# The last chunk of a weight stream: one load of 128 rows, or 14 loads of fewer than 16

## The chip, the cores and the metric

The kernel runs on one core of a Trainium2 chip. The metric is the device time of one execution in microseconds (us): 745.53 for the kernel before, the median of 3 runs (745.52 to 745.61).

## The reference

One decode step of a block in which attention and a gated layer stand side by side and are added to the residual, all in float32, for one token of 576 numbers:

```python
xn = _layernorm(x)
q = xn @ wq                                        # 32 heads of 128
p = softmax(einsum(q, k_cache) * 128 ** -0.5)      # 8192 cached keys for each head
A = einsum(p, v_cache).reshape(1, 1, 4096) @ wo    # 4096 x 576
gate, up = xn @ W_gate, xn @ W_up                  # 576 x 4608 each
h = gate * (gate > 0) * up
return x + A + h @ W_down                          # 4608 x 576
```

The caches are 2 x 32 x 8192 x 128 floats, 268 MB; with the weights the core reads 319 MB.

## The kernel before

Three big buffers of 128 partitions x 16384 floats (`slots`) are filled in turn by loads that SP issues in one queue, in the order in which they stand in `build`: the query weights, part of the gate weights, then for each head one load with its keys and the values of the head before it, then the last values with the rest of the gate weights (`vw`), and last the output weights (`wod`). VectorE multiplies the keys by the query and sums them (L292, L297), ScalarE takes the exponents (L311), and TensorE multiplies the values by them (L221). Each load waits until its buffer is free: `load` (L160) hands the waits to `add`, and `run` (L92) puts them ahead of the instruction on its engine.

The output stage multiplies one row by the 68 chunks of `wod`, each of 128 rows x 576 columns: 32 for the heads (`wo`), 36 for the gated layer (`W_down`). A chunk's rows lie on the 128 partitions, one row of 576 floats (2304 bytes) each. Chunks 0 to 8 come with `vw`. The others come in eight loads, whose sizes in chunks stand in `OUT` (L25): 28 into one buffer, 9, 7, 5, 4 and 3 into the next, 2 and 1 into the third. So the load of 3 brings chunks 62 to 64, that of 2 brings 65 and 66, and that of 1 brings chunk 67, the last. These two go into a buffer that is free when TensorE has done with the last head's values, with the gate products of the last part (`u3`) and with chunk 8 (`first`); SP's waits for all three are waits on TensorE's one counter, so one wait on the latest.

Each load has a semaphore of its own (`do65`, `do67`), to which a landed load has added 16; TensorE waits on it ahead of the first product of the load's first chunk (L404). Chunks 0 to 63 go in two halves each into the sums `acc`. When they are through, VectorE adds the residual (`y`, L422). The last four chunks go in four quarters each into `fin`; behind chunk 64 four products with `pick` bring `y` into the same sums, so TensorE waits for `y` there (L420). Then come chunks 65, 66 and 67, the copy of `fin` (L423) and the store of the 576 numbers (L185), which SP issues behind all loads.

In the profile, every matrix product and its weight load stand twice, as these are float32: the 4 products of a chunk's quarters are 8 rows. The 16 DMA engines that carry the loads aren't listed one by one; a view by stretches of time has their mean busy share.

Of the kernel before, what the change touches and what calls it, by code (L numbers as in the profile page):

```python
# [9 lines left out]
P = 128  # L10
D = 576
H = 32
# [4 lines left out]
FC = F // P  # L17
# [10 lines left out]
Q = D // 4  # L28

UNITS = (28, 32, 16, 5)  # L30


STEP = 16
# [4 lines left out]
class Program:  # L38
# [19 lines left out]
    def add(self, engine, f, waits=(), mark=None, on=None, by=1):  # L58
        to = None
        if mark is not None:  # L60
            to = on or engine
            self.sem(to)
            self.counts[to] += by
            assert mark not in self.marks, mark
            self.marks[mark] = (to, self.counts[to])
        self.lists[engine].append((f, tuple(waits), to, by))
# [41 lines left out]
def build(nc, x, kv, vw, wq, wqt, wg, wod, out):  # L108
    pr = Program(nc)
    add = pr.add  # L110

    def sb(name, shape):
        return nc.alloc_sbuf_tensor(name, list(shape), F32).ap()
# [4 lines left out]
    slots = [sb(f"slot{i}", [P, W]) for i in range(3)]  # L118
# [41 lines left out]
    def load(name, k, src, waits, on, start=0):  # L160
        dst = slots[k % 3][:, start:start + src.shape[-1]]
        add("sync", lambda e: e.dma_start(dst, src), waits, name, on=on, by=16)  # L162

    def tile(n):
        return slots[(n + 3) % 3]
# [11 lines left out]
    f = OUT[0][0]  # L177
    for k, loads in enumerate(OUT[1:]):
        free = ((("V", H - 3), ("mr", H - 2)), (("V", H - 2), ("mr", H - 1)), (("V", H - 1), "u3", ("first", OUT[0][0] - 1)))[k]
        i = 0  # L180
        for n in loads:
            load(("o", f), H + 4 + k, wod[:, (f - 9) * D:(f - 9 + n) * D], free, f"do{f}", i * D)
            i += n
            f += n
    add("sync", lambda e: e.dma_start(out.rearrange("o (j q) -> (o j) q", j=4), total4[0:P:32, :]), ("end",), "out", on="dout", by=16)  # L185
# [34 lines left out]
    def mm(waits, mark, o, lhsT, rhs, start, stop):  # L220
        add("tensor", lambda e: e.matmul(o, lhsT, rhs, start=start, stop=stop), waits, mark)  # L221
# [5 lines left out]
    for k in range(36):  # L227
        if k < 32:
            r, a, j = k // 16, k // 4 % 4, k % 4
# [25 lines left out]
    units += [(a, r, 0) for a in range(4) for r in (4, 5)] + [(4, 4, 0)]  # L255
    assert len(units) == sum(UNITS)
    first, last = {}, {}
# [5 lines left out]
    def gates(part):  # L263
        t, there = places[part]
        for u in range(UNITS[part]):
            k = sum(UNITS[:part]) + u
            a, r, j = units[k]
            mm((there, "qr") if u == 0 else (), f"u{part}" if u == UNITS[part] - 1 else None,
               bq[32 * j:32 * j + 32, :], xz[:, a, 5 - r:37 - r] if a < 4 else xt[:, 5 - r:37 - r],
# [71 lines left out]
    for n in range(1, H):  # L341
        k, i = (n - 1) // G, (n - 1) % G
# [52 lines left out]
    f, end = 0, H + FC  # L395
# [3 lines left out]
    for k, loads in enumerate(OUT):  # L399
        t = tile(H)[:, SK + UNITS[3] * 512:] if k == 0 else slots[(H + 3 + k) % 3]  # L400
        i = 0
        for n in loads:
            for m in range(n):
                waits = (("o", f),) if m == 0 and k else ()  # L404
                waits += needs.get(f, ())
                if f < end - LAST:
                    for j in range(2):
                        r = 64 * (f % 2) + 32 * j
# [75 lines left out]
```

## Time and profile before

| what | value |
|---|---|
| median of the runs | 745.53 us |
| the profiled execution, first to last instruction (span) | 744.4 us |
| read from HBM | 319.16 MB, 429 GB/s over the span |
| busy: PE, DVE, ACT | 40%, 78%, 5% of the span |
| issue of chunk 67's load to its landing | 25.9 us |
| copy of the result (L423) begins | 742.40 us |

Of the profiled execution the profile gives the span; the 1.1 us between it and the median lie around the first and the last instruction. PE is TensorE's products, PEld its weight loads, DVE VectorE, ACT ScalarE, SP the engine that issues the loads; an SPq row is the issue of a DMA. In a row of the timeline the first number is the start in us from the span's beginning, the second the time from the first to the end of the last of the instructions that were merged (x how many), and the bracket tells how long the engine had been idle before them and who let it go on.

### The profile page before, as it was taken

How to read it: one execution, taken by the hardware profiler on the slowest of the kernel's cores; microseconds unless marked ns; L12 is line 12 of the kernel's file. 1: busy time of each engine (PE TensorE's matmuls, PEld its weight loads, DVE VectorE, ACT ScalarE, POOL GpSimd, SP SyncE). 2: the span in 40 equal slices, each digit the busy share in tenths (PEclk: the TensorE clock that was granted, in tenths of full speed). 3: DMA queues.
4: the chain of work that ended last, by engine and by line, in shares of the span. 5: the costliest groups of instructions: out<-in, count | busy, mean ns of one | idle time of the engine just before them, and what ended most of it. 6: DMA issues, size and time to landing. Idle time of an engine off the chain costs nothing.

```text
span 744.4 us, 4100 instructions
## 1 busy us (share of the span) xinstructions
PE 296.1 (40%) x1772; PEld 86.0 (12%) x1772; DVE 577.1 (78%) x178; ACT 36.1 (5%) x113; POOL 2.1 (0%) x10
## 2 busy tenths in 40 slices
PE   1554413252343343343344334324324324334676
PEld 1111100010010010010010001001001001001122
DVE  2000189989999999999999999999999999999610
ACT  1000001010010010010000000001001000000000
POOL 1000000000000000000000000000000000000000
PEclk9967755656565565666666666666566566566689
DMA  9999999999999999999999999999999999999997
GB/s 395 451 438 408 445 412 441 440 440 416 444 447 405 447 440 412 444 440 433 426 440 444 412 444 440 412 447 440 419 437 440 440 419 441 444 412 438 435 409 320
DMA packets 6360, 319.30 MB, mean 429 GB/s; under 512 B 711, under 2 KB 717, under 8 KB 1102
## 3 DMA queue, kind: packets, MB, share of 16 engines
q1 hardware_dynamic: 6344, 319.17, 99.3%
q8 instruction: 6, 0.10, 0.0%
q14 instruction: 4, 0.03, 0.0%
q10 hardware_dynamic: 6, 0.00, 0.0%
HBM read 319.16 MB, written 0.00 MB: 429 GB/s over the span
## 4 chain that ended last, share of the span: by engine, by line
DMA 53%; DVE 40%; PE 4%; issue 3%; SPq 0%; ACT 0%; DVEq 0%; ACTq 0%
DMA slot<-in_kv 43%; DVE slot L292 20%; DVE s L297 19%; DMA slot<-in_wqt 5%; DMA slot<-in_wod 5%; PE bank L221 4%; DVE mr L298 0%; DVE nb L301 0%; DVE os L305 0%; SPq L162 0%; DVE rl L304 0%; ACT row L315 0%; DVE x L422 0%; ACT pzs L311 0%; DVEq L102 0%
## 5 line engine op out<-in xcount | busy, mean ns | idle before, releaser
L292 DVE TENSOR_TENSOR slot<-slot,bank 128x8192 f32<-128x8192 f32 x32 | 277.9, 8685 | 82.9 <-PE bank L221 52.4
L297 DVE TENSOR_REDUCE s<-slot 128x64 f32<-128x8192 f32 x32 | 277.6, 8675 | 0.0
L221 PE MATMUL bank<-slot,pzs 128*12 128x512 f32 x1024 | 184.3, 886 | 207.0 <-ACT pzs L311 207.0
L221 PEld LDWEIGHTS bank<-slot,pzs 128*12 128x12 f32 x1024 | 35.2, 123 | 333.5 <-issue 333.3
L221 PE MATMUL bank<-slot,xz 128*32 128x512 f32 x208 | 37.6, 754 | 32.2 <-DMA slot<-in_wq 12.6
L221 PE MATMUL bank<-l,ones 128*128 128x3 f32 (+1 forms) x22 | 6.3, 355 | 99.6 <-ACT pzs L311 99.6
L221 PE MATMUL bank<-ident,mr 128*128 128x128 f32 x64 | 16.3, 338 | 73.6 <-DVE mr L298 73.6
L311 ACT ACTIVATE pzs<-s,nb 128x64 f32<-128x64 f32 x32 | 11.1, 348 | 462.6 <-issue 423.3
L242 DVE TENSOR_SCALAR row<-bank 128x512 f32<-128x512 f32 x1 | 0.7, 690 | 33.7 <-PE bank L221 33.7
L422 DVE TENSOR_TENSOR x<-bank,x 128x288 f32<-128x288 f32 x1 | 0.5, 457 | 27.2 <-PE bank L221 27.2
L221 PEld LDWEIGHTS bank<-ident,mr 128*128 128x128 f32 x64 | 9.9, 194 | 96.5 <-DVE mr L298 96.5
L221 PEld LDWEIGHTS bank<-l,ones 128*128 128x128 f32 x22 | 5.3, 300 | 102.4 <-ACT pzs L311 101.6
L279 ACT ACTIVATE dq<-ident,qs 128x128 f32<-128x128 f32 x32 | 10.7, 392 | 129.4 <-PE bank L221 89.5
L221 PEld LDWEIGHTS bank<-slot,xz 128*32 128x32 f32 x208 | 8.6, 134 | 58.5 <-issue 24.1
L221 PE MATMUL bank<-sel,row 128*128 128x3 f32 (+1 forms) x88 | 11.6, 254 | 7.9 <-ACT row L315 7.9
L221 PE MATMUL bank<-slot,os 128*1 128x288 f32 x128 | 10.9, 483 | 5.0 <-DMA slot<-in_wod 5.0
L221 PEld LDWEIGHTS bank<-sel,row 128*128 128x128 f32 x88 | 10.6, 191 | 17.4 <-ACT row L315 17.4
L221 PE MATMUL bank<-slot,hh 128*1 128x288 f32 (+1 forms) x160 | 10.5, 381 | 3.5 <-DMA slot<-in_wod 3.5
L221 PE MATMUL bank<-dq,ones 128*128 128x384 f32 (+1 forms) x24 | 11.1, 549 | 0.0
L221 PE MATMUL bank<-slot,xt 128*32 128x512 f32 x26 | 6.6, 991 | 9.3 <-DMA slot<-in_wqt 9.3
L315 ACT COPY row<-bank 128x512 f32<-128x512 f32 x11 | 6.4, 586 | 73.2 <-PE bank L221 73.2
L301 DVE TENSOR_REDUCE nb<-bank 128x1 f32<-128x128 f32 x32 | 9.0, 283 | 0.7 <-PE bank L221 0.7
(52 smaller groups left out, 53.1 us busy)
## 6 DMA issues: line engine op xcount, KB each, us to landing
slot<-in_wod SPq DMA_DIRECT2D x1, 8064.0 KB, 39.3
slot<-in_vw SPq DMA_DIRECT2D x1, 7968.0 KB, 39.6
slot<-in_wod SPq DMA_DIRECT2D x1, 2592.0 KB, 25.9
slot<-in_wod SPq DMA_DIRECT2D x1, 2016.0 KB, 30.3
slot<-in_wod SPq DMA_DIRECT2D x1, 1440.0 KB, 33.3
slot<-in_wod SPq DMA_DIRECT2D x1, 1152.0 KB, 35.6
slot<-in_wod SPq DMA_DIRECT2D x1, 864.0 KB, 36.9
slot<-in_wod SPq DMA_DIRECT2D x1, 576.0 KB, 25.6
```

Of the source, the lines that this page charges most:

```text
L221: add("tensor", lambda e: e.matmul(o, lhsT, rhs, start=start, stop=stop), waits, mark)
L242: add("vector", lambda e: e.tensor_scalar_mul(row, bq, SCALE), ("pq", "n7"), "qr")
L279: add("scalar", lambda e, m=m, h=h: e.activation(dq[:, m, :], ident, AF.Copy, scale=qs[:, h:h + 1]), (free,) if m == 0 else (), ("dq", k) ...
L292: add("vector", lambda e: e.tensor_mul(k3, k3, qb[:, m, None, :].to_broadcast([P, C, DH])), waits, ("mul", h))
L297: add("vector", lambda e: e.reduce_sum(s, k3, axis=AX.X), (("mul", h),), ("sum", h))
L301: add("vector", lambda e: e.tensor_reduce(nb[h % 2], pm, axis=AX.X, op=ALU.max, negate=True), (("pm", h),), ("nb", h))
L311: add("scalar", lambda e: e.activation(pz[:, i, :, 4 * G - 4:4 * G], s2[h % 2].rearrange("p (c b) -> p c b", b=4), AF.Exp, bias=nb[h % 2], ...
L315: add("scalar", lambda e: e.copy(row, bo), (("V", h),) + ((("ot", k - 1),) if k else ("pqt",)), ("oc", k), on="oc", by=STEP)
L422: add("vector", lambda e: e.tensor_add(x2, acc[:, :N2], x2), ("sums", "x2"), "y")
```

## The change

The load of chunk 67 (`f == H + FC - 1`) is cut by rows. `SPLIT` has the 14 sizes, 15, 14, and so on down to 3, and then 11, together 128. All of them stand at the same place of SP's list, each with the same wait (`free`), and all add to the semaphore `do67`. TensorE waits ahead of chunk 67 for the last of them, that is for 14 x 16 = 224 on this semaphore, where it waited for 16. Nothing else changes.

```diff
+SPLIT = (15, 14, 13, 12, 11, 10, 9, 8, 7, 6, 5, 4, 3, 11)
...
         for n in loads:
-            load(("o", f), H + 4 + k, wod[:, (f - 9) * D:(f - 9 + n) * D], free, f"do{f}", i * D)
+            if f < H + FC - 1:
+                load(("o", f), H + 4 + k, wod[:, (f - 9) * D:(f - 9 + n) * D], free, f"do{f}", i * D)
+            else:
+                r = 0
+                for rows in SPLIT:
+                    dst = slots[(H + 4 + k) % 3][r:r + rows, i * D:(i + 1) * D]
+                    add("sync", lambda e, dst=dst, src=wod[r:r + rows, (f - 9) * D:(f - 8) * D]: e.dma_start(dst, src), free,
+                        ("o", f) if r + rows == P else ("part", r), on=f"do{f}", by=16)
+                    r += rows
             i += n
             f += n
```

On SP, at the end of the programme, these rows stand in the kernel before (partitions x floats of each partition; `s_tensor` is TensorE's counter, `s_vector` VectorE's):

```order
L162 DMA slot<-in_wod 128x2304 [waits s_vector,s_tensor]
L162 DMA slot<-in_wod 128x1728 [waits s_vector,s_tensor]
L162 DMA slot<-in_wod 128x1152 [waits s_tensor]
L162 DMA slot<-in_wod 128x576 [waits s_tensor]
L185 DMA out_y<-total 4x144 [waits s_vector]
```

After the change there stand in the place of the row 128x576 fourteen rows; the first eleven of them, behind the load of chunks 65 and 66:

```order
L164 DMA slot<-in_wod 128x1152 [waits s_tensor]
L190 DMA slot<-in_wod 15x576 [waits s_tensor]
L190 DMA slot<-in_wod 14x576 [waits s_tensor]
L190 DMA slot<-in_wod 13x576 [waits s_tensor]
L190 DMA slot<-in_wod 12x576 [waits s_tensor]
L190 DMA slot<-in_wod 11x576 [waits s_tensor]
L190 DMA slot<-in_wod 10x576 [waits s_tensor]
L190 DMA slot<-in_wod 9x576 [waits s_tensor]
L190 DMA slot<-in_wod 8x576 [waits s_tensor]
L190 DMA slot<-in_wod 7x576 [waits s_tensor]
L190 DMA slot<-in_wod 6x576 [waits s_tensor]
L190 DMA slot<-in_wod 5x576 [waits s_tensor]
```

Rows 4x576, 3x576 and 11x576 and the store follow; the store has moved behind 13 more issues. On PE, the end of the programme after the change, which reads as before but for the line's number:

```order
L231 MATMUL bank<-slot,hh 1x144 [waits s_vector]
L231 MATMUL bank<-slot,hh 1x144 x3
L231 MATMUL bank<-x,pick 1x144 [waits s_vector]
L231 MATMUL bank<-x,pick 1x144 x3
L231 MATMUL bank<-slot,hh 1x144 [waits s_do65]
L231 MATMUL bank<-slot,hh 1x144 x7
L231 MATMUL bank<-slot,hh 1x144 [waits s_do67]
L231 MATMUL bank<-slot,hh 1x144 x3
```

These are chunk 64, the products with `pick`, chunks 65 and 66, and chunk 67. Nothing has moved here; only the count that is waited for on `do67` has grown.

## Prediction

> **What bounds the kernel now.** I read the page's header, its slices and its chain first.
>
> ```profile
> span 744.4 us, 4100 instructions
> DMA  9999999999999999999999999999999999999997
> GB/s 395 451 438 408 445 412 441 440 440 416 444 447 405 447 440 412 444 440 433 426 440 444 412 444 440 412 447 440 419 437 440 440 419 441 444 412 438 435 409 320
> DMA 53%; DVE 40%; PE 4%; issue 3%; SPq 0%; ACT 0%; DVEq 0%; ACTq 0%
> ```
>
> The 16 DMA engines are busy at nine tenths or more in every slice but the last. The kernel runs as fast as its bytes arrive, and no byte is added or taken away by this change. What can move is only the tail, in which the engines run out of work. So the second view is the chain of waits at its end.
>
> ```profile
> 702.90 36.89 DMA slot<-in_wod
> 739.79 0.04 issue
> 739.84 0.71 PE bank L221 x8
> 740.54 0.02 issue
> 740.57 0.47 DVE x L422
> 741.04 0.04 issue
> 741.08 1.30 PE bank L221 x32
> 742.38 0.02 issue
> 742.40 0.31 DVE total L423
> ```
>
> The chain's last DMA is not the load that the change splits. It is the load of chunks 62 to 64, whose landing frees PE at 739.84. After it come the last sums (PE), the add y (DVE, L422), the pick products and chunks 65 to 67 (PE), the copy (DVE, L423) and the store. The timeline shows how close the split load, that of chunk 67, comes to this chain.
>
> ```profile
> 741.08 0.10 PEld L221 LDWEIGHTS bank<-x,pick 128*1 128x1 f32 x8 [0.66 <-DVE x L422]
> 741.20 0.47 PEld L221 LDWEIGHTS bank<-slot,hh 128*1 128x1 f32 x16
> 741.32 1.01 PE L221 MATMUL bank<-slot,hh 128*1 128x144 f32 x24
> 741.90 0.11 PEld L221 LDWEIGHTS bank<-slot,hh 128*1 128x1 f32 x8 [0.23 <-DMA slot<-in_wod]
> 742.74 0.65 SPq L185 DMA_DIRECT2D out_y<-total  x1
> ```
>
> The 16 weight loads at 741.20 are chunks 65 and 66: no idle time stands before them. The 8 at 741.90 are chunk 67, and before them the weight port sat idle for 0.23 us, until the load of chunk 67 had landed. These **0.23 us** are all that an earlier landing of this load can give: with the load long there, chunk 67 would begin at 741.67, and everything behind it would move by as much. They are 0.03% of the time. About 0.2%, or 1.49 us of 745.53, is what a measurement of this kernel can tell from no change.
>
> **The change part by part.** *The issues.* SP issues one load fewer of 128 rows and 14 small ones. The issues now:
>
> ```profile
> core 0 of [0], span 744.4 us
> start us, us, engine line op out<-in xcount [idle before <-releaser]
> 700.65 2.57 SPq L162 DMA_DIRECT2D slot<-in_wod  x5
> ...
> 715.54 0.80 SPq L162 DMA_DIRECT2D slot<-in_wod  x2
> slot<-in_wod SPq DMA_DIRECT2D x1, 576.0 KB, 25.6
> slot<-in_wod SPq DMA_DIRECT2D x1, 288.0 KB, 25.9
> L197 ACTq DMA_DIRECT2D row<-in_x x1: 531/531/531, 0.7 to 0.7; - x1
> L198 ACTq DMA_DIRECT2D x<-in_x x1: 578/578/578, 1.8 to 1.8; - x1
> ```
>
> Five issues took 2.57 us, 0.51 each; two took 0.80. The loads of few rows (x, 1 and 2 rows) took 0.53 and 0.58, and the store of 4 rows 0.65. So 13 issues more cost SP between 13 x 0.40 = 5.2 and 13 x 0.65 = 8.5 us; I take 0.51, 6.6 us. The wait ahead of each is on one count of PE that has been reached when the first passes, so it holds nobody. Behind them on SP stands only the store, which waits for the copy at 742.40. The second of the two issues, that of chunk 67, begins near 715.9 and ends at 716.34, so the last of the 14 ends near 723 (725 at the dear end). The cover is the backlog: this load lands 25.9 us after its issue, because the earlier chunks are served first. As shown below, no engine reaches it before about 738.7, so 15 us are left: the issues cost **nothing** on the path, and would begin to cost at over 15.7/13 = 1.2 us more for each.
>
> *The service by the 16 engines.* The tail in half microseconds, where the last three columns are the granted clock, the mean busy share of the engines, and what they moved:
>
> ```profile
> 730.00:735.00 5.00, 3.65 (x64) 1.78 (x56) 0.00 (x0) 0.00 (x0) 0.00 (x0) 1.00 1.00 416
> 738.50:739.00 0.50, 0.36 (x8) 0.00 (x0) 0.00 (x0) 0.00 (x0) 0.00 (x0) 1.00 0.94 373
> 739.00:739.50 0.50, 0.00 (x0) 0.00 (x0) 0.00 (x0) 0.00 (x0) 0.00 (x0) 1.00 0.94 369
> 739.50:740.00 0.50, 0.17 (x4) 0.10 (x8) 0.00 (x0) 0.00 (x0) 0.00 (x0) 1.00 0.62 244
> 740.00:740.50 0.50, 0.50 (x16) 0.21 (x8) 0.00 (x0) 0.00 (x0) 0.00 (x0) 1.00 0.41 161
> 740.50:741.00 0.50, 0.25 (x8) 0.00 (x0) 0.43 (x1) 0.00 (x0) 0.00 (x0) 1.00 0.34 134
> 741.00:741.50 0.50, 0.42 (x16) 0.36 (x20) 0.03 (x1) 0.00 (x0) 0.00 (x0) 1.00 0.07 28
> 741.50:742.00 0.50, 0.50 (x21) 0.25 (x16) 0.00 (x0) 0.00 (x0) 0.00 (x0) 1.00 0.00 0
> ```
>
> The engines don't end together. From 739.4 or so the share falls: some end there, about five are busy until 741.0, and one or two until some 741.4. Full, they move 416 GB/s, 26.0 GB/s each. A row of chunk 67 has 2304 bytes, so it costs an engine 2304/26.0 = **0.089 us**. Of 128 rows each engine has 8, 0.71 us. The earliest engine therefore begins chunk 67 near 739.4 - 0.71 = 738.7, and the latest near 741.4 - 0.71 = 740.7.
>
> With loads of fewer than 16 rows the shares become unequal. The trace doesn't say which engine gets which row. If each of the n rows of a load goes to an engine of its own, an engine gets between 0 and 14 rows of the 14 loads, 0 to 1.24 us, where it had 8. The ends for the landing of chunk 67 follow: if the latest engine gets none or few, it is done with its part of chunks 65 and 66 and holds nobody up, and the 0.23 us go; if the latest engine gets 14, it ends 6 x 0.089 = 0.53 us later than now. In between lies an even deal, 8 rows, which changes nothing. I take +0.1, near the middle of -0.23 and +0.53. The same latest engine must not be slowed in chunks 65 and 66 either, since those have no slack: the load landed 25.6 us after 715.54, at 741.14, and PE took it at 741.20.
>
> The Trainium skill, "DMA: Bandwidth & Descriptors", section "Why a DMA increments its semaphore by 16 and not by 1", says that such a load runs on the lowest-numbered engines, as many as the largest number up to 16 that divides its rows. By it the shares are 14, 14, 14, 13, 12, 11, 10, 9, 8, 7, 6, 4, 3, 2, 1 and 0 rows from engine 0 up, and the result hangs on whether the high-numbered engines are the late ones; no row here names an engine.
>
> *The programme.* Some 13 more DMA instructions and their waits may have to be fetched. The page lists what fetching costs now.
>
> ```profile
> q8 instruction: 6, 0.10, 0.0%
> q14 instruction: 4, 0.03, 0.0%
> ```
>
> One packet of q8 is 0.10 MB/6, some 17 KB, or 0.64 us of one engine. I take no further one; at the worst one falls on the latest engine in the tail and adds 0.64.
>
> *The sum.* 744.4 us of span and 745.53 - 744.4 = 1.1 us around it give the median, so the profiled execution stands for the runs. Issues 0, service +0.1 (from -0.23 to +0.53), fetch 0 (to +0.64): **745.6**, from 745.3 to 746.7.
>
> **The rivals.** *Small loads are not served back to back, and it gets slower.* The 14 loads put neighbouring rows in the same moment into neighbouring partitions, and there are 14 landings to be signalled in place of one. What speaks against a price per load: chunks 65 and 66 landed at 741.14 and chunk 67 at 715.9 + 25.9 = 741.8, so the last load added 0.7 us, what its 8 rows cost each engine, and no fixed cost between two loads of one queue shows. But all of these loads have 128 rows, and one signal for eight rows of an engine; so I keep this rival below one in six, not at nothing. Take it that four neighbouring rows must go one after the other, so that every load takes 4 x 0.089 = 0.36 us. Fourteen take 5.0 us; begun at 738.7 they end at 743.7 in place of 741.4, and all behind is 2.3 us later: **747.8**. It decides from where chunk 67 lands 1.5 us later: (741.4 + 1.5 - 738.7)/14 = 0.30 us for each load of one row per engine, over three times what the rows give.
>
> The Trainium skill has two rules that speak against the change. "SBUF — State Buffer", section "Door 1: The DMA port swizzle", says that partitions 0 to 15 reach four of 16 ports, with 104 GB/s measured; by that figure 295 KB would take an estimated 2.8 us, which from 738.7 ends at 741.5, near today's end, and from a middle start at 739.5 ends 0.9 us later, giving 746.4. The trace has no transfer of 15 partitions that shows it. The other, under "Rules for kernel authors" in the DMA page, is that transfers under 64 KB are mostly overhead; no run here shows a load so small behind others, and the back-to-back landing of the last two speaks for an overhead that a queue hides.
>
> *The queue is too short.* Before, at most 8 of these loads are out at a time; after, 21. If 8 were the limit, seven issues would wait for the landings up to 741.14 and six for those of the split loads themselves, so two more round trips, of about 1 us each as the store's from 743.4 to the span's end: 747.5. It decides below some 14 loads. The second issue of the two at 715.54, with 8 out, wasn't held.
>
> *The change doesn't do what it says:* a small load isn't spread at all and one engine carries it, and in the end all 128 rows. That is 128 x 0.089 = 11.4 us from 738.7 to 750.1, 8.7 us later than now: 754.2.
>
> *Faster by over 1.49 us* would need earlier chunks to land earlier, whose bytes and places in the queue don't change.
>
> **How the numbers follow.** The forecast, within 0.2%, has 0.78; small loads served one by one 0.14; the short queue 0.03; no spread 0.03; faster 0.02. The prediction is the forecast's 745.6. Its own bounds are 745.3 to 746.7, with 0.78; to hold 8 in 10 the range takes in the nearest part of the first rival, which begins at 747.0, up to 747.2, and 0.1 below the least: 745.2 to 747.2. Faster 0.02, same 0.78, slower 0.20.
>
> **What would show it.** In the profile after, SP's issues on the split line should stand between 715.9 and 725, at 0.33 to 0.65 us each. The DMA share in the last half microseconds should fall later and more steeply if the rows went to the early engines, or trail past 741.5 if to the late ones. The idle time before chunk 67's weight load, 0.23 us now, should be gone in the one case and grow by up to 0.53 us in the other. Over 1.5 us of it, with an idle or half-busy DMA ahead, would be the first rival; SP issues behind 738 the second. The prediction is wrong if chunks 65 and 66, or anything ahead of 739.8, moves by more than some tenths.

## The result: 2.8 us slower, and the profile after

The changed kernel takes 748.40 us (median of 5 runs, 748.05 to 748.51) where the kernel before takes 745.56 (5 runs, 745.52 to 746.23): a ratio of 1.0035, with a 95% interval of 1.0024 to 1.0045. The forecast was 745.6, within 745.2 to 747.2; the time lies 1.2 us above the range.

The slices of the changed kernel differ little from those of before but for the last, in which 255 GB/s are moved instead of 320. The fetches of instructions are the same six and four packets.

```profile
span 747.0 us, 4113 instructions
DMA  9999999999999999999999999999999999999996
q8 instruction: 6, 0.10, 0.1%
q14 instruction: 4, 0.03, 0.0%
```

The chain of waits of the changed kernel, its last pieces: it now ends with the split load. The last DMA before was the one of chunks 62 to 64.

```profile
724.11 20.07 DMA slot<-in_wod
744.19 0.04 issue
744.23 0.70 PE bank L231 x8
744.93 0.02 issue
744.96 0.31 DVE total L433
```

Chunk 62's first weight load in the timeline of the kernel before, a row that the prediction does not show:

```profile
739.83 0.59 PEld L221 LDWEIGHTS bank<-slot,hh 128*1 128x1 f32 x16 [1.54 <-DMA slot<-in_wod]
```

The timeline of the changed kernel, to be held against this row and those of before at 741.20, 741.90 and 742.40:

```profile
716.84 7.56 SPq L190 DMA_DIRECT2D slot<-in_wod  x14
739.89 0.59 PEld L231 LDWEIGHTS bank<-slot,hh 128*1 128x1 f32 x16 [1.97 <-DMA slot<-in_wod]
741.80 0.35 PEld L231 LDWEIGHTS bank<-slot,hh 128*1 128x1 f32 x16 [0.56 <-DMA slot<-in_wod]
744.23 0.11 PEld L231 LDWEIGHTS bank<-slot,hh 128*1 128x1 f32 x8 [2.08 <-DMA slot<-in_wod]
744.96 0.31 DVE L433 COPY total<-bank 128x144 f32<-128x144 f32 x1 [3.88 <-PE bank L231]
```

Two waits are new. Chunks 65 and 66, which had no idle time before them, now wait 0.56 us for their load, and this load has not been touched. Chunk 67 waits 2.08 us where it waited 0.23. From chunk 62's first weight load to chunk 65's it takes 741.80 - 739.89 = 1.91 us instead of 741.20 - 739.83 = 1.37, and on to chunk 67's 744.23 - 741.80 = 2.43 instead of 0.70. Where the 2.56 us between the two copies (744.96 and 742.40) come from is then: 0.06 from chunk 62's start, 0.54 from chunks 65 and 66, 1.73 from chunk 67, and 0.23 from its products, 0.73 to the copy instead of 0.50, under a lower granted clock (0.54 in the last row below). The span is 2.6 us longer, the median 2.8.

The tail of the changed kernel in half microseconds, with clock, DMA share and GB/s in the last three columns:

```profile
741.50:742.00 0.50, 0.26 (x12) 0.18 (x12) 0.00 (x0) 0.00 (x0) 0.00 (x0) 1.00 0.08 28
742.00:742.50 0.50, 0.47 (x16) 0.13 (x8) 0.00 (x0) 0.00 (x0) 0.00 (x0) 1.00 0.04 14
742.50:743.00 0.50, 0.00 (x0) 0.00 (x0) 0.00 (x0) 0.00 (x0) 0.00 (x0) 1.00 0.00 0
743.50:744.00 0.50, 0.00 (x0) 0.00 (x0) 0.00 (x0) 0.00 (x0) 0.00 (x0) 1.00 0.00 0
744.00:744.50 0.50, 0.27 (x8) 0.11 (x8) 0.00 (x0) 0.00 (x0) 0.00 (x0) 0.54 0.00 0
```

By these records the engines stop moving bytes before 742.5, two slices or about 1 us later than before. Yet the load counts as landed only at 744.19, 1.7 us or more later. Before, the bytes ended before 741.5 and the landing was waited for until 741.90. So most of the loss stands where no bytes are moved. Over 1.5 us of wait ahead of chunk 67, with an idle DMA, is the sign that the prediction had named for its first rival. The trace also has each engine's report of a landed load (an addition to the load's semaphore) and each packet moved. Eight of the last eleven reports on `do67` stand 0.18 us apart, from 742.91 to 744.19: one engine reports its loads one by one, at twice the 0.089 us that a row's bytes take. The last packets of rows, by contrast, follow each other every 0.095 us, and the last begins at 742.21. So the time is lost behind the moving of the bytes, not between one load's bytes and the next's.

### The profile page after: what moved, and what is told of

Read it like the earlier page. It is cut to its first block, busy times and chain, and to the rows that moved or that the text cites. A ratio compares the mean times of both kernels' runs of the same rounds, so it can differ in the third digit from the quotient of the medians.

```text
span 747.0 us, 4113 instructions
## 1 busy us (share of the span) xinstructions
PE 293.5 (39%) x1772; PEld 87.1 (12%) x1772; DVE 577.1 (77%) x178; ACT 36.1 (5%) x113; POOL 2.1 (0%) x10
## 4 chain that ended last, share of the span: by engine, by line
DMA 51%; DVE 43%; PE 5%; SPq 1%; issue 0%; ACT 0%; DVEq 0%; ACTq 0%
DMA slot<-in_kv 43%; DVE slot L302 21%; DVE s L307 21%; DMA slot<-in_wqt 5%; PE bank L231 5%; DMA slot<-in_wod 3%; SPq L190 1%; DVE mr L308 1%; DVE nb L311 0%; SPq L164 0%; DVE os L315 0%; ACT row L325 0%; DVEq L104 0%; DVE rl L314 0%; DVE total L433 0%
## 5 line engine op out<-in xcount | busy, mean ns | idle before, releaser
L231 PE MATMUL bank<-slot,pzs 128*12 128x512 f32 x1024 | 177.7, 857 | 204.1 <-ACT pzs L321 204.1
L231 PE MATMUL bank<-ident,mr 128*128 128x128 f32 x64 | 19.5, 395 | 80.0 <-DVE mr L308 80.0
L231 PEld LDWEIGHTS bank<-ident,mr 128*128 128x128 f32 x64 | 12.0, 235 | 101.4 <-DVE mr L308 101.4
```

## The experiments

Three theories were set against each other. **Landing:** each load that an engine takes part in costs it some 0.09 us besides a one-row load's bytes; the thought was that its landing is reported on its own. **Deal:** loads of fewer than 16 rows go to the low-numbered engines, and one of these is the latest. **Place** (first "neighbours"): rows for partitions that another engine is just writing hold that engine up. The yardstick in the profiles is the time from chunk 62's first weight load to chunk 65's and to chunk 67's; the first shows what the untouched load of chunks 65 and 66 loses, the second all that the split costs ahead of chunk 67. Each ratio is taken with runs of the kernel before made beside it (medians 745.56 to 745.76) and is not the plain quotient of the medians.

| kernel | 62 to 65 | 62 to 67 | time, us | ratio, 95% interval |
|---|---|---|---|---|
| before | 1.37 | 2.07 | 745.56 | |
| the change | 1.91 | 4.34 | 748.40 | 1.0035 (1.0024 to 1.0045) |
| 8 x 16 rows, neighbours | hidden | 2.99 | 747.08 | 1.0019 (1.0009 to 1.0028) |
| 8 x 16 rows, apart | 1.95 | 3.42 | 747.30 | 1.0020 (1.0011 to 1.0030) |
| 77, 49 and 2 rows | 1.94 | 2.95 | 746.86 | 1.0015 (1.0005 to 1.0024) |
| before, four probes | 1.39 | 2.09 | 745.64 | one run |
| the change, watched | 1.68 | 4.06 | 747.86 | one run |
| before, 13 small loads ahead | hidden | 4.16 | 747.81 | 1.0026 (1.0016 to 1.0035) |
| before, more rows apart | 1.38 | 2.09 | 745.74 | one run |
| before, more rows, neighbours | 4.70 | 5.67 | 749.66 | one run |
| 112 rows, 5 x 3 and 1 | 1.95 | not apart | 746.87 | 1.0011 (1.0002 to 1.0021) |
| 4 x 144 columns | 1.41 | 2.29 | 746.34 | 1.0007 (0.9997 to 1.0017) |
| the change, rotated | 1.83 | 4.23 | 747.96 | 1.0028 (1.0018 to 1.0038) |
| before, small neighbours | 3.44 | 4.12 | 748.06 | 1.0028 (1.0018 to 1.0039) |

"Hidden" means that PE was still busy with chunk 64 and `pick`, under a lower clock, when the load had landed. There the reports serve instead: from the last for chunk 62's load to the last for chunk 65's both runs take 1.52 us, where the kernel before takes 1.37.

**Eight loads of 16 rows, neighbours.** An even deal with eight landings:

```diff
-SPLIT = (15, 14, 13, 12, 11, 10, 9, 8, 7, 6, 5, 4, 3, 11)
+SPLIT = (16,) * 8
```

> The last chunk by 8 loads of 16 neighbouring rows: one row for each of the 16 engines in each load, so 8 rows per engine as in the kernel before, but 8 landings in place of 1. Landing theory (each load costs every engine that carries a part of it about 0.085 us besides its rows, since the last landings stand 0.18 us apart and a row takes 0.09): chunk 67 is 0.6 us later than before, 746.2. Deal theory (only the number of rows on the latest engine counts): no change, 745.6. Neighbour theory (rows of neighbouring partitions wait for one another): at least as bad as the change, 748 or more.

Chunk 67 began 0.92 us later than before by the yardstick; by the reports 0.15 of it is in chunks 65 and 66 and 0.77 behind them. Not "at least as bad as the change", so nearness within a load isn't what costs; not nothing either, so the deal isn't all. In the time there are some tenths of slower products: from chunk 62's start to `y` PE took 1.2 us instead of 0.7.

**Eight loads of 16 rows, apart.**

```diff
-SPLIT = (15, 14, 13, 12, 11, 10, 9, 8, 7, 6, 5, 4, 3, 11)
+SPLIT = (16,) * 8
...
-                    dst = slots[(H + 4 + k) % 3][r:r + rows, i * D:(i + 1) * D]
-                    add("sync", lambda e, dst=dst, src=wod[r:r + rows, (f - 9) * D:(f - 8) * D]: e.dma_start(dst, src), free,
+                    dst = slots[(H + 4 + k) % 3][r // 16:P:8, i * D:(i + 1) * D]
+                    add("sync", lambda e, dst=dst, src=wod[r // 16:P:8, (f - 9) * D:(f - 8) * D]: e.dma_start(dst, src), free,
```

> As the run with 8 loads of 16 neighbouring rows, but each load takes every eighth row, so that the rows of a load lie 8 partitions apart. Landing theory: the same as with neighbours, 746.2. Neighbour theory: well below the run with neighbours, near 745.6. Deal theory: no change, 745.6.

Rows 8 partitions apart did no better than neighbours (747.30 and 747.08, intervals that overlap): the neighbour theory in its first form fell. The timeline of this run:

```profile
739.87 0.59 PEld L231 LDWEIGHTS bank<-slot,hh 128*1 128x1 f32 x16 [1.89 <-DMA slot<-in_wod]
741.82 0.35 PEld L231 LDWEIGHTS bank<-slot,hh 128*1 128x1 f32 x16 [0.60 <-DMA slot<-in_wod]
743.29 0.10 PEld L231 LDWEIGHTS bank<-slot,hh 128*1 128x1 f32 x8 [1.12 <-DMA slot<-in_wod]
```

From chunk 65's load to chunk 67's 1.47 us pass, for 8 loads of one row per engine: 0.184 each. With the same 8 rows in one load it was 0.70. That is the landing theory's price, 0.77/8 = 0.10 us per load. The last packet of the loads ends at 741.82, the last report comes at 743.25: here too the price is paid behind the bytes. But chunks 65 and 66 are late by 0.58 us as well, which the theory doesn't explain, and with neighbours by 0.15 only; why these two differ is not shown.

**Three loads of 77, 49 and 2 rows.**

```diff
-SPLIT = (15, 14, 13, 12, 11, 10, 9, 8, 7, 6, 5, 4, 3, 11)
+SPLIT = (77, 49, 2)
```

> The last chunk by 3 loads of 77, 49 and 2 rows. If a load runs on as many engines as the largest number up to 16 that divides its rows, these are 11 engines with 7 rows, 7 with 7, and 2 with 1: engines 0 and 1 get 15 rows, 2 to 6 get 14, 7 to 10 get 7, the others none: the share of the low engines as after the change, with 3 landings in place of 14. Deal theory with a low-numbered engine the latest: 6 to 7 rows more at 0.09 and nothing else, 0.5 to 0.6 us, and all of the change's loss should come back if the deal were all of it: 748. Landing and deal together: 0.55 for the rows and 2 x 0.085 for the landings, 746.3. If the latest engine is a high-numbered one: 745.3.

With three landings, more than half of the change's loss is gone (1.0015 against 1.0035), though by the assumed deal engine 3 carries 14 rows. So the deal by itself, which would have brought all of the loss back (748), fell. From chunk 65 to chunk 67 it took 1.01 us instead of 0.70: 0.31 for the six rows more, less than the 0.53 that 0.089 each would be. Chunks 65 and 66 are 0.57 late all the same: this delay doesn't need many small loads.

**Who is late.** Four more loads behind chunk 67's, and ScalarE as a clock:

```diff
+PROBES = (1, 2, 3, 12)
...
+    spare = slots[(H + 6) % 3]
+    for m, n in enumerate(PROBES):
+        add("sync", lambda e, m=m, n=n: e.dma_start(spare[:n, (4 + m) * D:(5 + m) * D], wod[:n, :D]), free, ("probe", m), on=f"probe{m}", by=16)
...
+    for m, n in enumerate(PROBES):
+        add("scalar", lambda e, m=m, n=n: e.copy(spare[:n, 12 * D + m:12 * D + m + 1], spare[:n, (4 + m) * D:(4 + m) * D + 1]), (("probe", m),), "watched" if m == len(PROBES) - 1 else None)
```

> The kernel before, with four more loads of 1, 2, 3 and 12 rows into a spare place behind the load of chunk 67, each with a semaphore, on which ScalarE waits in turn with a small copy; the store waits for the last of them. The copies' starts are a clock: if the latest engine is the lowest-numbered one, even the load of 1 row lands behind chunk 67, near 742.1; if it is the second or third, the first copy starts about 1 to 2 us earlier, near 740.0, and the second or third behind 742; if it is among the higher ones, only the last, of 12 rows, is late or none.

Its timeline, the copies and chunk 67's weight load:

```profile
739.94 0.19 ACT L431 COPY slot<-slot 1x1 f32<-1x1 f32 x1 [29.65 <-DMA slot<-in_wod]
740.64 0.36 ACT L431 COPY slot<-slot 2x1 f32<-2x1 f32 x2 [0.51 <-DMA slot<-in_wod]
741.74 0.10 PEld L226 LDWEIGHTS bank<-slot,hh 128*1 128x1 f32 x8 [0.26 <-DMA slot<-in_wod]
741.91 0.19 ACT L431 COPY slot<-slot 12x1 f32<-12x1 f32 x1 [0.91 <-DMA slot<-in_wod]
```

The one row has landed by 739.94, and the last reports of the loads of 2 and 3 rows come at 740.61 and 740.78; the load of 12 rows follows chunk 67 by 0.17 us. So loads of 1, 2 and 3 rows run on engines that are early, and the latest is among the next nine.

**The change, watched.**

```diff
+WATCHED = (0, 42, 84, 114)
...
-                        ("o", f) if r + rows == P else ("part", r), on=f"do{f}", by=16)
+                        ("o", f) if r + rows == P else ("part", r), on=f"w{r}" if r in WATCHED else f"do{f}", by=16)
...
+                waits += tuple(("part", r) for r in WATCHED) if f == end - 1 else ()
...
+    for r in WATCHED:
+        add("scalar", lambda e, r=r: e.copy(spare[:3, 12 * D + r:12 * D + r + 1], spare[:3, 13 * D:13 * D + 1]), (("part", r),), "watched" if r == WATCHED[-1] else None)
```

> The changed kernel, but the loads of 15, 11, 7 and 3 rows (the 1st, 5th, 9th and 13th) have semaphores of their own, on which ScalarE waits in turn with small copies; the products of chunk 67 wait for all of them and the common semaphore. The copies' starts are a clock. Landing theory: the last engine puts its rows down 0.18 us apart, so the four starts stand about 4 x 0.18 = 0.7 us apart, from near 742 to 744, long after the engines' bytes stop (742.3). If instead the rows are all there and only the last signal is late: the first three start together, near 742. The time as for the change, 748.4.

The expectation names the watched loads wrongly: those at rows 0, 42, 84 and 114 are the 1st, 4th, 8th and 13th, of 15, 12, 8 and 3 rows.

```profile
741.71 0.19 ACT L440 COPY slot<-slot 3x1 f32<-3x1 f32 x1 [29.95 <-DMA slot<-in_wod]
742.29 0.19 ACT L440 COPY slot<-slot 3x1 f32<-3x1 f32 x1 [0.39 <-DMA slot<-in_wod]
743.01 0.28 ACT L440 COPY slot<-slot 3x1 f32<-3x1 f32 x2 [0.53 <-DMA slot<-in_wod]
743.92 0.10 PEld L233 LDWEIGHTS bank<-slot,hh 128*1 128x1 f32 x8 [2.04 <-DMA slot<-in_wod]
```

From the 1st load to the 4th 0.58 us pass (0.19 each), to the 8th 0.72 (0.18 each). The 13th, of 3 rows, was there by then: it wasn't waited for, and its last report came at 742.22. The loads of 7, 6, 5, 4 and 11 rows still came, 0.91 us, 0.18 each; the last five reports on `do67` are 0.18 apart. So the loads are reported one by one, and the latest engine takes part in the load of 4 rows and not in that of 3: if the engines are dealt from the lowest up, it is the fourth, engine 3, with 13 of the 14 loads. The semaphores agree on the number: the load of 12 rows was reported by 12 engines, that of 8 by 8, that of 3 by 3. This is the number of engines that the Trainium skill, "DMA: Bandwidth & Descriptors", section "Why a DMA increments its semaphore by 16 and not by 1", gives; that they are the lowest-numbered ones, as it also says, the traces can't show, but the late engine's place among them fits it.

**Thirteen small loads ahead of a whole one.**

```diff
+                for m in range(13):
+                    add("sync", lambda e, m=m: e.dma_start(spare[0:P:8, (4 + m) * D:(4 + m) * D + 128], wod[0:P:8, :128]), free, ("small", m), on=f"do{f}", by=16)
             load(("o", f), H + 4 + k, wod[:, (f - 9) * D:(f - 9 + n) * D], free, f"do{f}", i * D)
```

> The kernel before with its whole load of chunk 67, and 13 more loads of 16 rows (every eighth) of 512 bytes into a spare place ahead of it, on the same semaphore, so 14 landings for every engine and an even deal. Landing theory: 13 x (0.09 for the landing + 0.02 for the bytes) = 1.4 us later on every engine, also on the latest one: 747.0. If landings are free and rows alone count: 13 x 0.02 = 0.3, 745.9. If a landing costs more the more bytes the row has, something between.

```profile
739.66 0.38 PEld L225 LDWEIGHTS bank<-slot,hh 128*1 128x1 f32 x12 [1.63 <-DMA slot<-in_wod]
743.82 0.11 PEld L225 LDWEIGHTS bank<-slot,hh 128*1 128x1 f32 x8 [1.60 <-DMA slot<-in_wod]
```

Chunk 67 began 4.16 us after chunk 62, 2.09 more than before. By the reports 0.15 of it is in chunks 65 and 66, and behind them chunk 67 took 2.64 instead of 0.70: 0.15 for each load of 512 bytes per engine, of which the bytes would be 0.02. The landing's price stands alone here: the deal is even, and the rows are a quarter as long. It was expected at 0.09 + 0.02; it is larger, and a row of 2304 bytes raises it only to 0.18. So price and bytes don't simply add.

**More rows, apart and as neighbours.** The kernel before with two loads of 4 rows of 16 KB behind chunk 67's, waited for at the very end only; in the one to partitions 0, 4, 8 and 12, in the other to 12 to 15:

```diff
+    for m in range(2):
+        add("sync", lambda e, m=m: e.dma_start(spare[0:16:4, (4 + 8 * m) * D:(4 + 8 * m) * D + 4096], kv[0, 0:16:4, :4096]), free, ("more", m), on="more", by=16)
...
+    nc.sync.wait_ge(pr.sems["more"], 32)
```

> The kernel before with two more loads behind chunk 67's, each of 4 rows of 16 KB into a spare place, rows 0, 4, 8 and 12; nobody but the end of the programme waits for them. Engines 0 and 2, which are early, carry them while the latest engine still works at chunks 65 to 67. If what delays chunks 65 and 66 by 0.6 us in the split kernels is that an early engine writes to partitions another engine is just writing, and if the four rows here are on four different engines' partitions: chunk 67 lands as before, near 741.8. If any traffic of the early engines delays the late one: near 742.4.

> As the run with four rows apart, but the two loads go to partitions 12 to 15, four neighbours that in a load of 128 rows belong to one engine, by the split kernels' landings probably the latest one. If early engines' writes there take turns with that engine's: chunk 67 lands 0.5 to 1 us later than in the run with rows apart, near 742.5. If place doesn't matter: the same in both.

The neighbours:

```profile
739.87 0.59 PEld L224 LDWEIGHTS bank<-slot,hh 128*1 128x1 f32 x16 [1.53 <-DMA slot<-in_wod]
744.57 0.58 PEld L224 LDWEIGHTS bank<-slot,hh 128*1 128x1 f32 x16 [3.35 <-DMA slot<-in_wod]
```

Apart, nothing moved: chunk 67 began 2.09 us after chunk 62. As neighbours, these loads, which are behind chunks 65 to 67 in every queue, held chunks 65 and 66 up by 4.70 - 1.37 = 3.33 us, far more than the 0.5 to 1 us expected. By the reports they held up one engine above all: 15 of the 16 engines had reported chunks 65 and 66 by 742.07, the last came at 744.53. Six of the rows belong to engines 0 to 2 by the deal, and at 26.0 GB/s each takes 0.63 us: 3.8 in all, 0.5 more than measured. The two kernels differ in nothing but the rows' places, on the chip and also in the memory read from; no run parts these two. So place matters, with the same bytes, each shown by one run.

**Early engines only.**

```diff
-SPLIT = (15, 14, 13, 12, 11, 10, 9, 8, 7, 6, 5, 4, 3, 11)
+SPLIT = (112, 3, 3, 3, 3, 3, 1)
```

> The last chunk by a load of 112 rows (16 engines, 7 rows each), 5 loads of 3 rows and one of 1: by the deal that the runs so far showed, only engines 0 to 2 carry the small loads, of which 0 and 2 are early, and the late engine 3 has one row less. If the deal were all: chunk 67 lands 0.09 us earlier than before, 745.5. Landing theory: the same, since the early engines have 1 to 2 us for 6 x 0.18 us. Place theory (a row that an early engine writes to the late engine's partitions, 12 to 15 and 44 to 47, holds that engine up): in a load of 112 rows these belong to engines 1, 2 and 6, so chunks 65 and 66 land up to 0.5 us later, and the time is 745.7 to 746.3.

The late engine has one row less and no small load; chunks 65 and 66 are late by 0.58 us, as the place theory has it, and the kernel is 0.1% slower (1.0011). The median, 746.87, is above that theory's 746.3; the last products ran under a granted clock of 0.51. Chunk 67 followed chunks 65 and 66 without a wait of its own. So not even the deal that suits the engines gains here.

**By columns.**

```diff
-SPLIT = (15, 14, 13, 12, 11, 10, 9, 8, 7, 6, 5, 4, 3, 11)
+SPLIT = (144,) * 4
...
-                    dst = slots[(H + 4 + k) % 3][r:r + rows, i * D:(i + 1) * D]
-                    add("sync", lambda e, dst=dst, src=wod[r:r + rows, (f - 9) * D:(f - 8) * D]: e.dma_start(dst, src), free,
-                        ("o", f) if r + rows == P else ("part", r), on=f"do{f}", by=16)
+                    dst = slots[(H + 4 + k) % 3][:, i * D + r:i * D + r + rows]
+                    add("sync", lambda e, dst=dst, src=wod[:, (f - 9) * D + r:(f - 9) * D + r + rows]: e.dma_start(dst, src), free,
+                        ("o", f) if r + rows == D else ("part", r), on=f"do{f}", by=16)
```

> The last chunk by 4 loads of 128 rows and 144 columns (576 bytes a row): 4 landings, the even deal, and every engine on the partitions that it has in all loads of 128 rows. Place theory: chunks 65 and 66 land as before, 741.2. Landing theory with a price that adds to the rows, 0.09 to 0.14 us each: chunk 67 lands 0.3 to 0.4 us later than before, 745.9. If the landing's price is hidden wherever an engine has several rows in a load: 0 to 0.2 us later, 745.7.

```profile
739.59 0.59 PEld L231 LDWEIGHTS bank<-slot,hh 128*1 128x1 f32 x16 [1.53 <-DMA slot<-in_wod]
741.00 0.44 PEld L231 LDWEIGHTS bank<-slot,hh 128*1 128x1 f32 x16
741.88 0.11 PEld L231 LDWEIGHTS bank<-slot,hh 128*1 128x1 f32 x8 [0.44 <-DMA slot<-in_wod]
```

Chunks 65 and 66 wait for nothing again: where all loads have 128 rows, none of them is held up. Chunk 67 is 0.22 us later by the yardstick, for three landings more: 0.07 each, where it was 0.15 in the 13 small loads. With 8 rows per engine in each load most of the price is hidden. The time itself can't be told from no change (0.9997 to 1.0017).

**Rotated.**

```diff
-SPLIT = (15, 14, 13, 12, 11, 10, 9, 8, 7, 6, 5, 4, 3, 11)
+SPLIT = (15, 14, 13, 12, 11, 9, 6, 10, 8, 7, 5, 4, 3, 11)
...
-                r = 0
+                r = 48
...
-                        ("o", f) if r + rows == P else ("part", r), on=f"do{f}", by=16)
-                    r += rows
+                        ("o", f) if r + rows == 48 else ("part", r), on=f"do{f}", by=16)
+                    r = (r + rows) % P
```

> The changed kernel with the same 14 sizes in another order, and the first load at row 48 in place of 0, so that rows 12 to 15 and 44 to 47, the late engine's partitions, come in the last seven loads. Landings and deal as in the change. Place theory: chunks 65 and 66 land as before the change, near 741.2, and chunk 67 about 0.6 us earlier than with the change, 743.6 instead of 744.2: 747.8. If place doesn't matter: 748.4 as for the change.

Missed: chunks 65 and 66 were still 1.83 us behind chunk 62, not 1.4. As the change itself gave 1.91 and its watched copy 1.68, this run doesn't tell whether the order of the places matters. The rows for partitions 12 to 15 and 44 to 47 may still have come while engine 3 was writing; that was reckoned, not seen.

**Small neighbours.** The place theory with rows of the split's own size:

```diff
+    for m in range(8):
+        add("sync", lambda e, m=m: e.dma_start(spare[12:16, (4 + m) * D:(5 + m) * D], wod[12:16, :D]), free, ("more", m), on="more", by=16)
...
+    nc.sync.wait_ge(pr.sems["more"], 128)
```

> The kernel before with eight more loads behind chunk 67's, each of 4 rows of 2304 bytes, the split's own row size, into spare columns of partitions 12 to 15; nobody but the end of the programme waits for them. Engines 0 and 2 carry 16 of the 32 rows before the late engine 3 is done. Place theory with rows of this size: these 16 rows take turns with engine 3's, up to 16 x 0.089 = 1.4 us: chunks 65 and 66 are waited for, and chunk 67 begins 0.5 to 1.4 us later than before, near 742.9. If rows this small pass between the late engine's without holding it up: chunk 67 as before, near 741.9, and the delay of chunks 65 and 66 in the split kernels has another cause.

```profile
739.48 0.59 PEld L224 LDWEIGHTS bank<-slot,hh 128*1 128x1 f32 x16 [1.53 <-DMA slot<-in_wod]
742.92 0.35 PEld L224 LDWEIGHTS bank<-slot,hh 128*1 128x1 f32 x16 [2.10 <-DMA slot<-in_wod]
743.60 0.11 PEld L224 LDWEIGHTS bank<-slot,hh 128*1 128x1 f32 x8 [0.32 <-DMA slot<-in_wod]
```

Chunks 65 and 66 came 3.44 us after chunk 62, 2.07 more than before, for loads that nobody waits for and that stand behind in every queue. The rows of engines 0, 1 and 2 are 24, and 24 x 0.089 = 2.1. The expectation counted engines 0 and 2 only (16 rows, 1.4 us); with engine 1 the size fits. So small rows hold the late engine's load up as well; that they take turns with its rows one by one is argued from the size. By the reports it was again one engine above all: 15 of the 16 had reported chunks 65 and 66 by 741.65, the last came at 742.88. But several of the 15 were late too, by up to 0.9 us against the kernel before, counted from chunk 62's reports in their order, which partitions 12 to 15 don't explain. No run has the same eight loads elsewhere.

## Why the prediction was wrong

**The issues: right.** 14 issues took 7.56 us, 0.54 each on average instead of 0.51 (the longest 1.50), and were over at 724.40, 14 us before the first engine reported one of them. The rivals of a short queue and of a load that isn't spread are out: all loads were issued by 724.40, and 12 rows were reported by 12 engines.

**The fetches: right.** No further packet.

**The service by the engines: this is the step that failed.** It priced a row at 0.089 us, whatever load it comes in, and a load at nothing. The latest engine has 13 rows, in 13 loads, and the loads took 0.18 us each or a little more: 2.43 us from chunk 65 to chunk 67 instead of 0.70. Of the 1.73 us more, the deal (5 rows more at 0.089) is 0.45 by reckoning, inside the bounds given; the other 1.28 are the loads' own price, 0.10 for each of 13, and stood in no bound of the forecast. The even splits by 8 loads (0.184 each) and the 13 small loads (0.15) show that price without the deal; the watched run (0.18 to 0.19) shows it load by load. How the 1.73 is shared is less sure, as the three loads gave only 0.31 for six rows more. The prediction had looked for such a price and found none, as chunk 67 followed chunks 65 and 66 by what its 8 rows cost; the splits by columns show why that misled: with 8 rows per engine in a load most of the price is hidden (0.07). The price is paid behind the bytes; what takes that time is not shown.

**Chunks 65 and 66.** The prediction said that they have no slack and would make it wrong if they moved; it put no price on that. They moved by 0.54 us. A hold-up of this kind was shown beside the change, not in it: rows of early engines written to partitions 12 to 15 held the late engine's load up by 2.07 and 3.33 us, the bigger of these loads elsewhere by nothing, and splits by columns by nothing. The Trainium skill, "DMA: Bandwidth & Descriptors", section "The descriptor swizzle", gives partitions 12 to 15 and 44 to 47 to engine 3 in a load of 128 rows; the engine that was late and the partitions on which it could be held up agree with that. In the split, by the deal, seven of the eight rows of chunk 67 for these partitions are written by others (row 45 falls to engine 3 itself), 0.62 us if all come in engine 3's way. That this is the 0.54 is argued from sizes; rotating the order didn't settle it. Nor is engine 3 alone in it: in the changed kernel the last nine of the 16 reports of chunks 65 and 66 are each 0.4 to 0.6 us later than before, counted from chunk 62's reports in their order. If place does it, it does so on the partitions of all the late engines. The cause of this delay stays open.

**The first rival** had the right sign, named the landings, and its sign in the profile came true. That its time, 747.8, was nearly right is luck, as its price and its place were off. It let four neighbouring rows take turns, 0.36 us for each load, from the earliest engine's 738.7 on, and had the limit at 0.30 us per load. The early engines had time enough; rows 8 partitions apart did no better than neighbours; and what counts is the late engine, which begins when its part of chunks 65 and 66 is done. There 13 loads may cost 0.70 + 1.49 = 2.19 us before 0.2% is lost, 0.17 each, and 0.18 is over that by itself. The order of engines on which the gain hung was against the change too: the latest engine is the fourth from below and gets 13 rows.

**What was left to gain,** the 0.23 us of idle time ahead of chunk 67, was read rightly, and none of the splits tried got any of it: each paid in landings, or its chunks 65 and 66 came late.

## What to carry to other kernels

Price a small load at the engine that ends last, and per load, not per byte: behind others in a queue a load of one 2304-byte row per engine took 0.18 us, twice its bytes, while loads with 8 rows per engine hid most of that. Ask too where each engine's rows go: four loads of 128 rows held nothing up here, while rows dealt otherwise came with a delay of an earlier load on which someone waited, 0.15 to 0.58 us in the splits by rows. A levelling of engines can give at most what is waited for at the end, here 0.23 us, and this is to be weighed against both first.

## What the runs showed that was not expected

- A load can delay one that is ahead of it in every queue: eight loads of 4 rows of 2304 bytes behind chunk 67 delayed chunks 65 and 66 by 2.07 us.
- Bytes and landing can lie far apart: after the change no bytes are moved from 742.5 on, and the load lands at 744.19; before, the bytes ended before 741.5 and the wait at 741.90.
- The split delayed not one engine in chunks 65 and 66 but all that come late: the last nine reports by 0.4 to 0.6 us each, the first three by under 0.1.
